# Linear attention and a squared-ReLU feed-forward layer: fourteen entries that copy weights to DRAM taken out, four moved, and the written order of all engines from step 17 on replaced

## Chip, cores, metric

The kernel runs on one NeuronCore of a Trainium2 chip. The metric is the device time of one execution in microseconds (us). Before the change three executions took 855.23, 855.45 and 857.17 us, so the median is 855.45 us.

## What is computed

```python
q_s = softmax of q over the head dimension          # q, k, v: 8 batches x 8 heads x 576 rows x 64
k_s = softmax of k over the sequence
kv  = einsum('bhsd,bhse->bhde', k_s, v)
x   = einsum('bhsd,bhde->bhse', q_s, kv)            # becomes 4608 tokens x 512
h   = x @ w_in                                      # w_in: 512 x 2048
out = (maximum(h, 0) ** 2) @ w_out                  # w_out: 2048 x 512
```

## The kernel before

**Blocks and steps.** Each batch is a block of 512 tokens; the 64 left over of each batch make a ninth block. A block's hidden units are worked on in 16 steps of 128. Blocks 0 to 2 are done step by step (steps 0 to 47): `h{n}_{cc}` is a quarter of the first product of step n, `relu`, `rm`, `ghi`, `glo` square it and split it into a rounded part and a rest, `o.{n}.{t}` is a quarter of the second product. Each h and each o is three matmuls of 128x512, since a product of two split numbers takes three. Blocks 3 and 4, 5 and 6, 7 and 8 are then done two at a time, in passes `s0`, `s1`, `s2`. There seven products of sums and differences of quarter matrices (`A11`, `S4`, `S2`, `A12`, `S3`, `S1`, `A22`, six matmuls each, for each of eight pieces) take the place of eight.

**What pass s0 needs.** The weights that all passes use are written to DRAM tensors and read back into a ring of seven tiles (`refill`, entries `s0.R.n`). The first use of the tile comes 10 to 25 us of matmuls after its entry. `ko{fc}` in the first list and `keep.{fc}` in the second are one copy of 512 KB of w_out (line 970). `WA{j}` and `w{j}.WA` are three copies of 256 KB of w_in (line 1030). The two inputs of pass s0 come back from DRAM (`x0.LB11`, `LB12`, `LB21`, `LB22`), their differences are `x0.T1` to `x0.T4`, and VectorE, ScalarE and GpSimd split each (`l`, `h`, `p`).

**Attention by pairs of heads.** A block has four pairs, written b.p (`2.1` is pair 1 of block 2). For a pair, `Lq`, `Lk`, `Lv` load it (two, two and four DMAs), `qm` to `qy` make the softmax of q, `tb` turns 32x32 pieces, `Bw` writes the result to one of two DRAM buffers `bounce` and `B` brings it back transposed as `qT` in four DMAs. `qh0`, `qh1` round the two heads' `qT` on ScalarE, `ql0`, `ql1` make the rests on GpSimd. `km`, `k1`, `k2`, `ke`, `kx` make the exponentials of k, `kv`, `kr`, `kh`, `kl` the small matrix, and `P0` to `P3` are the matmuls whose sums (`c`, `d`) are x. `XL` and `XR` store parts of x. In the first list the same things are called `Bw20`, `B20`, `qh20`, `kh20`, `kl20` and so on. `S0` to `S3` there store block 0's output, and `Lq23` loads the q of pair 2.3.

**The order.** Nothing is scheduled by a program. `ORDER` (line 51) covers the start up to step 17, `LIST` (line 92) the rest. Each entry issues its instructions, and every engine and the DMA queue of SyncE (SP) takes its own in exactly this order, since each instruction is issued after the one before it on the same engine:

```python
class InOrder:
    ...
                if self.last is not None:
                    order.enter_context(self.tc.issue_after(self.last.ins))
                ins = f(*args, **kwargs)
...
    def keep_out(fc):
        e.sp.dma_start(w_outs[fc], wo[fc].bitcast(F32))
...
    for token in LIST:
        run(token)
```

In the lists of before, `ORDER` copies w_out's chunks 0, 1, 2, 3, 4, 6, 7, 8 and w_in's groups 0 to 5, and `LIST` copies all thirteen and all eight.

Of the kernel before, what the change touches and what calls it, by code (L numbers as in the profile page):

```python
# [103 lines left out]
w0.h34 o.21.3 d0/2.2 B/2.3 h24_0 ghi23 P1/2.2 glo23 h24_1 c1/2.2 h24_2 w0.h12 d1/2.2 w4.WA w0.l34 xh0/2.2 P2/2.2
h24_3 c2/2.2 xl0/2.2 o.22.0 d2/2.2 relu24 tb/3.0 w0.l12 P3/2.2 w0.W34 o.22.1 rm24 k1/3.0 o.22.2 c3/2.2 qd/3.1
qh0/2.3 o.22.3 d3/2.2 w0.W12 h25_0 ghi24 ql0/2.3 kv/2.3 xh1/2.2 glo24 qh1/2.3 h25_1 kr/2.3 Bw/3.0 qx/3.1 xl1/2.2
h25_2 Lq/3.3 kh/2.3 ql1/2.3 qs/3.1 h25_3 o.23.0 Lv/3.1 relu25 o.23.1 kl/2.3 rm25 qy/3.1 k2/3.0 P0/2.3 o.23.2 c0/2.3
o.23.3 w1.a2 d0/2.3 h26_0 ghi25 tb/3.1 B/3.0 P1/2.3 h26_1 w1.s1 glo25 c1/2.3 h26_2 d1/2.3 kp/2.3 kz/3.0 ke/3.0
xh0/2.3 h26_3 Lk/3.1 P2/2.3 qm/3.2 xl0/2.3 o.24.0 relu26 Bw/3.1 o.24.1 w1.a1 rm26 XL/2.2 o.24.2 c2/2.3 qd/3.2 XL/2.3
kx/3.0 d2/2.3 o.24.3 qm/3.3 w3.WA P3/2.3 w1.s2 h27_0 ghi26 c3/2.3 glo26 h27_1 w1.s3 qh0/3.0 d3/2.3 h27_2 Lq/4.0  # L110
km/3.1 ql0/3.0 xh1/2.3 kv/3.0 qx/3.2 h27_3 Lv/3.2 kr/3.0 xl1/2.3 o.25.0 qs/3.2 relu27 w1.s4 o.25.1 rm27 o.25.2
k1/3.1 w1.h34 qy/3.2 o.25.3 w1.h12 B/3.1 h28_0 w1.l34 kp/3.0 ghi27 kz/3.1 h28_1 kh/3.0 glo27 w1.l12 h28_2 qm/4.0
w1.W34 h28_3 kl/3.0 o.26.0 w2.a1 relu28 P0/3.0 Lk/3.2 k2/3.1 rm28 o.26.1 c0/3.0 o.26.2 w1.W12 tb/3.2 P1/3.0 o.26.3
qh0/3.1 ke/3.1 h29_0 ghi28 w2.a2 Bw/3.2 h29_1 c1/3.0 glo28 XL/3.0 kx/3.1 h29_2 km/3.2 XR/3.0 ql0/3.1 h29_3 kv/3.1
relu29 k1/3.2 w1.WA w2.s1 o.27.0 rm29 o.27.1 w2.s2 kr/3.1 o.27.2 Lv/3.3 w2.s3 k2/3.2 kh/3.1 o.27.3 w2.s4 h30_0 ghi29
kl/3.1 h30_1 w2.h34 qd/3.3 glo29 P0/3.1 w2.h12 B/3.2 h30_2 w2.l34 kp/3.1 c0/3.1 h30_3 qx/3.3 w3.a1 P1/3.1 relu30
qs/3.3 w2.l12 o.28.0 Lq/4.1 rm30 o.28.1 c1/3.1 ke/3.2 o.28.2 w2.W34 o.28.3 qh0/3.2 qy/3.3 h31_0 ghi30 w2.W12 h31_1
ql0/3.2 kx/3.2 glo30 h31_2 qm/4.1 kv/3.2 tb/3.3 Lk/3.3 h31_3 kr/3.2 qd/4.0 o.29.0 relu31 XR/3.1 o.29.1 rm31 Bw/3.3
w3.a2 o.29.2 qx/4.0 Lq/4.2 o.29.3 kh/3.2 qs/4.0 w3.s1 h32_0 ghi31 Lv/4.0 h32_1 glo31 qy/4.0 h32_2 km/3.3 h32_3 w3.s2
o.30.0 tb/4.0 w3.s3 relu32 B/3.3 o.30.1 rm32 qm/4.2 qd/4.1 o.30.2 k1/3.3 o.30.3 w3.s4 Bw/4.0 h33_0 ghi32 Lq/4.3  # L120
kp/3.2 h33_1 qx/4.1 glo32 h33_2 w3.h34 qs/4.1 Lk/4.0 h33_3 w3.h12 o.31.0 k2/3.3 qy/4.1 XL/3.1 relu33 o.31.1 ev.1.0.a
x0.LB11 o.31.2 w3.l12 rm33 st.1.0 ev.1.1.d o.31.3 tb/4.1 h34_0 ghi33 w3.W12 ev.1.3.d qd/4.2 h34_1 glo33 h34_2 w3.l34
qx/4.2 h34_3 Bw/4.1 kl/3.2 o.32.0 w3.W34 relu34 ke/3.3 P0/3.2 o.32.1 ev.1.2.a qs/4.2 rm34 o.32.2 Lq/5.0 kx/3.3
km/4.0 qy/4.2 o.32.3 h35_0 st.1.1 ghi34 h35_1 c0/3.2 glo34 w4.a2 h35_2 XL/3.2 qm/4.3 st.1.2 P1/3.2 h35_3 w4.a1
qh0/3.3 o.33.0 k1/4.0 st.1.3 relu35 ql0/3.3 o.33.1 rm35 o.33.2 tb/4.2 c1/3.2 w6.WA w4.s1 kv/3.3 k2/4.0 w4.s2 o.33.3
XR/3.2 h36_0 w4.s3 kr/3.3 ghi35 Lv/4.1 h36_1 kp/3.3 kh/3.3 glo35 qd/4.3 h36_2 qm/5.0 h36_3 w4.s4 qx/4.3 o.34.0
kl/3.3 relu36 Lk/4.1 o.34.1 ke/4.0 rm36 P0/3.3 w4.h34 qs/4.3 o.34.2 Lq/5.1 c0/3.3 o.34.3 w4.h12 w4.l34 P1/3.3 XL/3.3
ghi36 h37_0 w4.l12 w4.W34 kx/4.0 glo36 h37_1 c1/3.3 km/4.1 h37_2 qy/4.3 kv/4.0 w4.W12 tb/4.3 h37_3 kp/4.0 o.35.0
kr/4.0 qd/5.0 relu37 o.35.1 XR/3.3 k1/4.1 rm37 Lk/4.2 o.35.2 w5.a2 kh/4.0 qx/5.0 o.35.3 k2/4.1 Lv/4.2 h38_0 ghi37
w5.s1 h38_1 glo37 h38_2 w5.a1 h38_3 kl/4.0 o.36.0 ke/4.1 B/4.0 relu38 o.36.1 km/4.2 w5.s2 rm38 o.36.2 kx/4.1 w5.s3  # L130
o.36.3 Lq/5.2 k1/4.2 w5.s4 h39_0 ghi38 h39_1 w5.h34 glo38 x0.LB21 h39_2 w5.l34 qh0/4.0 Bw/4.2 h39_3 k2/4.2 w5.h12
w5.W34 ql0/4.0 o.37.0 relu39 o.37.1 rm39 ke/4.2 o.37.2 B/4.1 P0/4.0 w6.a1 o.37.3 qm/5.2 w5.l12 h40_0 ghi39 h40_1
kx/4.2 glo39 w7.WA w6.a2 h40_2 c0/4.0 qs/5.0 h40_3 P1/4.0 qm/5.1 w5.W12 o.38.0 qy/5.0 qh0/4.1 o.38.1 relu40 o.38.2
ql0/4.1 tb/5.0 rm40 Bw/4.3 o.38.3 c1/4.0 XL/4.0 kv/4.1 ghi40 XR/4.0 B/4.2 h41_0 glo40 kp/4.1 w6.s1 h41_1 kr/4.1
h41_2 kh/4.1 w6.s2 Lk/4.3 h41_3 kl/4.1 w6.s3 o.39.0 Lv/4.3 P0/4.1 w6.s4 o.39.1 c0/4.1 w7.a1 o.39.2 relu41 P1/4.1
o.39.3 c1/4.1 w2.WA qh0/4.2 km/4.3 h42_0 kv/4.2 rm41 ql0/4.2 k1/4.3 ghi41 h42_1 XR/4.1 w6.h34 h42_2 Lv/5.0 w6.h12
glo41 h42_3 w6.l12 kr/4.2 o.40.0 relu42 k2/4.3 o.40.1 rm42 qd/5.1 o.40.2 B/4.3 kh/4.2 x0.hB110 o.40.3 kl/4.2 kp/4.2
h43_0 ghi42 ke/4.3 P0/4.2 w6.W12 glo42 kx/4.3 h43_1 w6.l34 h43_2 c0/4.2 h43_3 w6.W34 P1/4.2 relu43 o.41.0 kz/5.0
qh0/4.3 o.41.1 c1/4.2 Lk/5.0 ql0/4.3 o.41.2 rm43 kv/4.3 x0.hB111 XR/4.2 o.41.3 x0.hB210 kp/4.3 kr/4.3 Bw/5.0 h44_0
w7.a2 ghi43 Lk/5.1 h44_1 kh/4.3 glo43 h44_2 kl/4.3 s0.R.0 w7.s1 h44_3 km/5.0 Lv/5.1 P0/4.3 w7.s2 o.42.0 k1/5.0  # L140
c0/4.3 w7.s3 o.42.1 w7.s4 P1/4.3 k2/5.0 o.42.2 kz/5.1 c1/4.3 x0.LB12 relu44 o.42.3 XR/4.3 w7.h12 ke/5.0 h45_0 Lq/5.3
rm44 h45_1 km/5.1 w7.l12 w7.h34 h45_2 XL/4.3 ghi44 XL/4.1 h45_3 w7.l34 x0.hB211 w7.W12 o.43.0 glo44 relu45 o.43.1
# [1163 lines left out]
```

## Time and profile before

| | |
|---|---|
| median of three executions | 855.45 us |
| the profiled execution | 856.13 us |
| its span from first to last instruction | 854.3 us |
| time around the span | 1.83 us |
| mean granted TensorE clock | 0.997 |
| TensorE busy / VectorE / ScalarE / GpSimd | 837.1 / 548.8 / 494.0 / 287.0 us |
| bytes moved by all DMAs | 188.58 MB |
| written to HBM | 54.00 MB |

The span is what the engines took; the 1.83 us lie around it. TensorE (PE) has 4286 matmuls. Waits in which it sat idle can be found stretch by stretch.

### The profile page before, as it was taken

What the parts mean: (1) busy time and instruction counts of PE and PEld (TensorE: products, weight loads), DVE (VectorE), ACT (ScalarE), POOL (GpSimd) and SP (SyncE); (2) the same over time, 40 slices, a digit from 0 to 9 for tenths busy, and PEclk for the clock granted to TensorE, in tenths of its full rate; (3) what the DMA queues carried; (4) which work ended last, traced back from release to release, by engine and by line L of the source; (5) the groups of instructions that cost most, each with busy time, mean ns of one, the idle gap of its engine ahead of it and who ended that gap; (6) DMA issues with size and microseconds to landing.
All of it is one profiled execution on the core that took longest, in us unless ns stands there. A gap on an engine that the chain in (4) does not pass through costs nothing.

```text
span 854.3 us, 13089 instructions
## 1 busy us (share of the span) xinstructions
PE 837.1 (98%) x4286; PEld 679.1 (79%) x4286; DVE 548.8 (64%) x1153; ACT 494.0 (58%) x934; POOL 287.0 (34%) x275
## 2 busy tenths in 40 slices
...
GB/s 228 284 185 307 273 259 269 357 282 216 237 229 218 257 245 270 296 265 246 254 242 253 264 203 210 251 203 176 173 222 197 117 209 146 167 168 155 181 66 49
DMA packets 162643, 188.58 MB, mean 221 GB/s; under 512 B 52112, under 2 KB 125328, under 8 KB 162576
## 3 DMA queue, kind: packets, MB, share of 16 engines
...
q10 hardware_dynamic: 752, 0.95, 0.4%
...
HBM read 133.69 MB, written 54.00 MB: 220 GB/s over the span
## 4 chain that ended last, share of the span: by engine, by line
PE 84%; DVE 5%; DMA 4%; ACT 2%; issue 2%; SPq 2%; POOL 1%; DVEq 0%; ACTq 0%; POOLq 0%
PE bank L295 84%; DMA qt<-in_q_dram 2%; SPq L295 2%; DMA kt<-in_k_dram 1%; DVE m L295 1%; DMA xl_B<-x_raw 1%; DMA qT<-bounce 1%; DVE T L295 1%; DVE w L295 1%; DVE bank L295 1%; ACT bank L295 1%; DVE g_lo L295 0%; POOL qn L295 0%; ACT g_hi L295 0%; ACT qs L295 0%
## 5 line engine op out<-in xcount | busy, mean ns | idle before, releaser
L295 PE MATMUL bank<-wp,g 128*128 128x512 f32 x648 | 160.7, 390 | 0.0
L295 PEld LDWEIGHTS bank<-wp,g 128*128 128x128 f32 x648 | 120.8, 188 | 25.4
L295 PE MATMUL bank<-xh_T,wp 128*128 128x512 f32 x384 | 132.2, 393 | 1.1 <-ACT bank L295 1.1
L295 PE MATMUL bank<-x_hi,wi 128*128 128x512 f32 x384 | 132.5, 398 | 0.0
L295 PE MATMUL bank<-wo,g_hi 128*128 128x512 f32 x384 | 121.9, 399 | 0.0
L295 POOL TENSOR_TENSOR qs<-qT,qs 64x640 fp32r<-64x640 f32 (+1 forms) x40 | 62.7, 1568 | 105.9 <-ACT qs L295 88.5
L295 PE MATMUL bank<-xh_B,wp 128*128 128x512 f32 x288 | 98.0, 391 | 0.0
L295 DVE TENSOR_TENSOR c<-c,bank 128x512 f32<-128x512 f32 x48 | 33.0, 687 | 83.5 <-ACT c L295 83.3
L295 PEld LDWEIGHTS bank<-xh_T,wp 128*128 128x128 f32 x384 | 72.1, 188 | 17.5 <-ACT bank L295 1.9
L295 PEld LDWEIGHTS bank<-x_hi,wi 128*128 128x128 f32 x384 | 72.3, 188 | 16.4 <-DVE x_lo L295 0.4
L295 ACT ACTIVATE far<-far 128x512 f32<-128x512 f32 x96 | 60.7, 633 | 40.3 <-DVE far L295 38.8
L295 PEld LDWEIGHTS bank<-wo,g_hi 128*128 128x128 f32 x384 | 70.9, 190 | 14.9 <-ACT g_hi L295 0.4
L295 PE MATMUL bank<-wo,g_lo 128*128 128x512 f32 x192 | 75.8, 395 | 0.0
L295 PE MATMUL bank<-x_lo,wi 128*128 128x512 f32 x192 | 75.0, 391 | 0.0
L295 PE MATMUL bank<-xl_T,wp 128*128 128x512 f32 x192 | 74.8, 390 | 0.0
L295 PE MATMUL bank<-wo_back,g 128*128 128x512 f32 x288 | 72.0, 390 | 0.0
L295 DVE TENSOR_TENSOR far<-far,bank 128x512 f32<-128x512 f32 x48 | 32.9, 685 | 54.5 <-PE bank L295 54.4
L295 PEld LDWEIGHTS bank<-xh_B,wp 128*128 128x128 f32 x288 | 54.1, 188 | 11.6
L295 PEld LDWEIGHTS bank<-wo_back,g 128*128 128x128 f32 x288 | 53.7, 188 | 11.3
L295 DVE TENSOR_TENSOR g<-far,g 128x512 fp32r<-128x512 f32 x48 | 34.0, 747 | 38.7 <-ACT g L295 38.5
L295 ACT CAST g<-far 128x512 fp32r<-128x512 f32 x48 | 27.7, 620 | 51.5 <-PE bank L295 51.2
L295 PE MATMUL bank<-xl_B,wp 128*128 128x512 f32 x144 | 56.3, 391 | 0.0
(135 smaller groups left out, 1529.8 us busy)
## 6 DMA issues: line engine op xcount, KB each, us to landing
wp<-w_outs SPq DMA_DIRECT2D x54, 512.0 KB, 4.3
wp<-w_sums SPq DMA_DIRECT2D x96, 256.0 KB, 3.6
wp<-w_own SPq DMA_DIRECT2D x72, 256.0 KB, 3.5
w_own<-wi SPq DMA_DIRECT2D x42, 256.0 KB, 3.0
w_outs<-wo SPq DMA_DIRECT2D x21, 512.0 KB, 4.6
...
raw_i<-in_moe_w_in_dram SPq DMA_DIRECT2D x16, 512.0 KB, 7.1
raw_o<-in_moe_w_out_dram SPq DMA_DIRECT2D x16, 512.0 KB, 7.2
```

The lines of the kernel that those rows point to most:

```text
L295: ins = f(*args, **kwargs)
```

## The change

Only the two lists change. `ORDER` loses `ko7`, `ko8` and `WA5`, `ko0`, `ko1` and `ko3` stand earlier and `ko6` later. `LIST` loses `keep.0`, `.1`, `.2`, `.3`, `.4`, `.6` and `w0.WA` to `w4.WA`. Each weight is then copied once: chunks 0, 1, 2, 3, 4, 6 and groups 0 to 4 in `ORDER`, the others in `LIST`. In `LIST` the same 2686 other entries stand in a new order; its last 429 entries are the same. `w5.WA`, `w6.WA`, `w7.WA` now stand between steps 21 and 22; before, w6 and w7 stood near steps 35 and 40.

```diff
 s2o10 hii12 loi12 relu11 Lo12 Lv20 lowi13 qs13 qadd13 ti13 kexp20 lowi14 Lo15 Lq21 o8_0 o9_0 s1i13 hio10 loo10 rs13
-rr13 kvn13 s2i13 rm11 lowo14 Lv21 WA0 WA1 to11 o8_2 o9_2 ghi10 ghi11 h12_0:0 h12_1 h12_2 h12_3 rc13 qmul13 s1o11
...
-h15_0:3 h15_1 h15_2 h15_3 Lv22 WA2 WA3 ko0 ko1 ko2 ghi13 relu14 to14 s1o14 s2o14 to15 glo13 o13_3 o13_1 o13_2 hio14
-loo14 o13_0 s1o15 s2o15 hio15 rm14 ghi14 glo14 h16_0:1 relu15 rm15 ghi15 glo15 Bw20 Lk23 WA4 ko3 ko4 ko6 ko7 o14_3
-qsub21 at13:3 loo15 o15_3 xhi13 xlo13 o14_0 o15_0 B20 rs20 h16_1 rr20 qexp21 ev3 S3 qn21 ev0 S0 WA5 ko8 Bw21 h16_2
-o14_1 o15_1 ev1 qh20 ql20 kf20 h16_3 relu16 rm16 ghi16 S1 B21 glo16 o14_2 o15_2 ev2 S2 kh20 kl20 Lq23 h17_0:3 h17_1
...
+rr13 kvn13 s2i13 rm11 lowo14 Lv21 WA0 WA1 ko0 ko1 to11 o8_2 o9_2 ghi10 ghi11 h12_0:0 h12_1 h12_2 h12_3 rc13 qmul13
...
+h15_0:3 h15_1 h15_2 h15_3 Lv22 WA2 WA3 ko2 ko3 ghi13 relu14 to14 s1o14 s2o14 to15 glo13 o13_3 o13_1 o13_2 hio14
+loo14 o13_0 s1o15 s2o15 hio15 rm14 ghi14 glo14 h16_0:1 relu15 rm15 ghi15 glo15 Bw20 Lk23 WA4 ko4 o14_3 qsub21 at13:3
+loo15 o15_3 xhi13 xlo13 o14_0 o15_0 B20 rs20 h16_1 rr20 qexp21 ev3 S3 qn21 ev0 S0 ko6 Bw21 h16_2 o14_1 o15_1 ev1
...
 LIST = """
-w0.a2 w0.s1 qm/2.2 P0/2.0 h18_0 relu17 km/2.2 qd/2.2 h18_1 rm17 h18_2 ghi17 c0/2.0 h18_3 glo17 qx/2.2 o.16.0 d0/2.0
-relu18 qs/2.2 P1/2.0 o.16.1 rm18 o.16.2 c1/2.0 qy/2.2 Lq/3.0 d1/2.0 o.16.3 k1/2.2 P2/2.0 h19_0 ghi18 keep.9 c2/2.0
-h19_1 glo18 xh0/2.0 keep.11 h19_2 xl0/2.0 d2/2.0 keep.0 tb/2.2 h19_3 keep.12 P3/2.0 keep.1 o.17.0 qm/2.3 relu19
-Bw/2.2 o.17.1 rm19 k2/2.2 qd/2.3 keep.13 o.17.2 c3/2.0 keep.15 o.17.3 d3/2.0 qx/2.3 Lq/3.1 ke/2.2 h20_0 ghi19 kv/2.1
-kx/2.2 glo19 keep.2 h20_1 keep.3 xh1/2.0 qs/2.3 qh0/2.1 xl1/2.0 Lv/2.3 h20_2 qh1/2.1 h20_3 kr/2.1 qy/2.3 o.18.0
-km/2.3 relu20 o.18.1 ql0/2.1 rm20 tb/2.3 o.18.2 keep.4 kh/2.1 keep.6 o.18.3 kp/2.1 Bw/2.3 kl/2.1 h21_0 ghi20 ql1/2.1
-keep.7 P0/2.1 glo20 h21_1 keep.8 c0/2.1 h21_2 XL/2.0 d0/2.1 k1/2.3 P1/2.1 h21_3 c1/2.1 o.19.0 d1/2.1 relu21 o.19.1
-k2/2.3 XL/2.1 rm21 P2/2.1 o.19.2 c2/2.1 xh0/2.1 o.19.3 d2/2.1 B/2.2 xl0/2.1 qm/3.0 P3/2.1 h22_0 ghi21 qd/3.0 c3/2.1
-glo21 h22_1 d3/2.1 h22_2 w0.WA ke/2.3 xh1/2.1 kv/2.2 xl1/2.1 kx/2.3 h22_3 kr/2.2 Lq/3.2 kp/2.2 o.20.0 w0.a1 relu22
-o.20.1 rm22 qm/3.1 w0.s2 Lk/3.0 o.20.2 qh0/2.2 w0.s3 o.20.3 kh/2.2 ql0/2.2 Lv/3.0 h23_0 ghi22 h23_1 qh1/2.2 glo22
...
-k2/5.1 kh/5.0 Lk/5.2 h46_3 o.44.0 kl/5.0 relu46 s0.R.2 x0.T10 o.44.1 rm46 Lv/5.2 x0.lB110 o.44.2 x0.hT10 o.44.3
...
-x0.hT11 x0.T31 o.46.2 o.46.3 x0.lT11 x0.hT31 s0.0.A11 x0.hB221 x0.pT40 glo47 back.0 o.47.0 x0.T21 x0.pB210 x0.hT21
-s0.0.c1 back.1 ev.2.0.a x0.lT21 st.2.0 x0.T41 s0.0.S2 kx/5.1 x0.lT31 x0.hT41 km/5.2 x0.pB211 s0.R.7 s0.0.u2 x0.pT41
...
+w0.a2 w0.s1 h18_0 relu17 qm/2.2 P0/2.0 h18_1 rm17 km/2.2 qd/2.2 h18_2 ghi17 h18_3 c0/2.0 glo17 o.16.0 relu18 d0/2.0
+o.16.1 km/2.3 rm18 P1/2.0 o.16.2 c1/2.0 o.16.3 qx/2.2 d1/2.0 Lq/3.0 P2/2.0 qs/2.2 ghi18 h19_0 c2/2.0 h19_1 keep.9
+xh0/2.0 glo18 keep.11 qy/2.2 h19_2 keep.12 d2/2.0 h19_3 keep.13 xl0/2.0 tb/2.2 P3/2.0 o.17.0 relu19 keep.15 k1/2.2
+o.17.1 Bw/2.2 rm19 keep.7 o.17.2 c3/2.0 qh0/2.1 keep.8 d3/2.0 o.17.3 qm/2.3 XL/2.0 ql0/2.1 kv/2.1 ghi19 xh1/2.0
+h20_0 glo19 Lv/2.3 qh1/2.1 qd/2.3 h20_1 k2/2.2 h20_2 xl1/2.0 qx/2.3 h20_3 k1/2.3 ql1/2.1 o.18.0 Lq/3.1 relu20 o.18.1
+kr/2.1 rm20 o.18.2 ke/2.2 kp/2.1 kh/2.1 B/2.2 o.18.3 k2/2.3 h21_0 ghi20 h21_1 kx/2.2 glo20 h21_2 w5.WA qs/2.3 h21_3
+o.19.0 relu21 kl/2.1 o.19.1 ke/2.3 rm21 P0/2.1 w6.WA o.19.2 qm/3.0 qy/2.3 c0/2.1 o.19.3 kx/2.3 d0/2.1 h22_0 tb/2.3
...
+glo44 h45_3 ke/5.1 o.43.0 x0.LB22 relu45 tb/5.1 o.43.1 rm45 x0.T10 Bw/5.1 o.43.2 kx/5.1 o.43.3 x0.lB110 x0.hT10
+h46_0 s0.R.1 ghi45 x0.lT10 h46_1 glo45 qd/5.2 h46_2 km/5.2 x0.hB220 h46_3 back.1 Lq/6.0 o.44.0 x0.T30 relu46 o.44.1
...
+x0.hT31 x0.lT11 B/5.0 o.46.0 ghi47 x0.lT31 o.46.1 glo47 x0.pT40 o.46.2 s0.R.5 o.46.3 x0.T21 s0.0.A11 x0.T41 x0.hT21
+x0.lT21 back.2 o.47.0 s0.0.c1 qs/5.2 x0.pB211 ev.2.0.a s0.0.S2 x0.hT41 st.2.0 k1/5.2 x0.pT41 s0.0.A12 s0.0.u2 s0.R.7
...
```

Some distances in the two lists, in the matmul time that stands between two entries (each matmul at the rate that the profile shows, three to an h or o, six to a product):

| from, to | before, us | after, us |
|---|---|---|
| B/2.2 to qh0/2.2 | 5.6 | 13.5 |
| start of LIST to qh0/2.2 | 29.1 | 30.5 |
| x0.LB22 to x0.T30 | 6.1 | 5.5 |
| start of LIST to x0.T30 | 177.7 | 173.7 |
| start of LIST to s0.0.S2 | 185.9 | 185.9 |
| Lk/6.1 to km/6.1 | 5.8 | 5.8 |
| Lk/5.0 to km/5.0 | 4.8 | 4.5 |
| Lk/5.1 to km/5.1 | 6.9 | 5.6 |
| Lk/7.1 to km/7.1 | 5.7 | 4.9 |
| Lq/6.3 to qm/6.3 | 15.5 | 4.3 |
| B/5.1 to Bw/5.3 | 7.5 | 3.4 |

In blocks 5 to 7, eight loads of k or q stand 7.0 us or less ahead of their first user before, and eleven after.

## Rows read from the trace of the kernel before

**Rows 1.** The page's first part: busy time of each engine.
```profile
PE 837.1 (98%) x4286; PEld 679.1 (79%) x4286; DVE 548.8 (64%) x1153; ACT 494.0 (58%) x934; POOL 287.0 (34%) x275
```

**Rows 2.** Busy time by stretch; after the engines: granted clock, DMA share, GB/s.
```profile
135.00:142.00 7.00, 5.60 (x26) 4.37 (x25) 4.14 (x8) 6.22 (x13) 5.24 (x5) 1.00 0.95 296
157.00:162.00 5.00, 3.53 (x16) 2.49 (x14) 4.80 (x11) 3.51 (x9) 4.51 (x5) 1.00 1.02 384
162.00:174.00 12.00, 12.00 (x71) 9.73 (x71) 7.65 (x22) 5.63 (x11) 4.53 (x6) 1.00 0.97 344
174.00:181.00 7.00, 3.18 (x13) 2.37 (x12) 2.45 (x3) 4.51 (x10) 3.62 (x3) 0.93 0.84 248
181.00:184.00 3.00, 3.00 (x9) 2.33 (x9) 2.90 (x6) 1.39 (x4) 1.43 (x2) 0.59 0.68 178
334.00:342.00 8.00, 6.83 (x29) 5.02 (x28) 7.17 (x15) 4.95 (x9) 2.99 (x4) 1.00 0.81 244
418.00:424.00 6.00, 4.91 (x23) 3.81 (x22) 4.47 (x15) 3.07 (x6) 0.00 (x0) 1.00 1.05 316
600.00:700.00 100.00, 100.00 (x443) 82.52 (x442) 43.69 (x62) 44.01 (x77) 9.15 (x6) 1.00 0.57 180
```

**Rows 3.** What PE waited for: us in total, times, longest.
```profile
PE bank L295 <- DVE kvs L295: 3.8, 1, 3.8
PE bank L295 <- POOL kt L295: 1.5, 1, 1.5
...
PE bank L295 <- DVE xr L295: 1.1, 1, 1.1
```

**Rows 4.** The chain that ended last: start, us, what.
```profile
148.50 3.06 DMA qt<-in_q_dram
...
174.68 2.10 DMA qT<-bounce
...
321.40 5.92 DMA xl_B<-x_raw
...
337.55 0.59 ACT bank L295
...
414.37 4.78 DMA kt<-in_k_dram
```

**Rows 5.** SP's queue in order of time: start, us of issuing, DMAs.
```profile
101.47 3.85 SPq L295 DMA_DIRECT2D w_own<-wi  x6
107.44 1.27 SPq L295 DMA_DIRECT2D qt<-in_q_dram  x2
...
126.76 4.00 SPq L295 DMA_DIRECT2D w_outs<-wo  x4
130.87 3.42 SPq L295 DMA_DIRECT2D qT<-bounce  x4
...
136.91 1.67 SPq L295 DMA_DIRECT2D w_own<-wi  x3
...
147.79 2.73 SPq L295 DMA_DIRECT2D qt<-in_q_dram  x4
150.57 4.41 SPq L295 DMA_DIRECT2D w_outs<-wo  x5
155.08 1.16 SPq L295 DMA_DIRECT2D bounce<-tb  x1
...
173.27 1.84 SPq L295 DMA_DIRECT2D qT<-bounce  x4
```

**Rows 6.** The page's DMA issues: KB each, us to landing.
```profile
w_own<-wi SPq DMA_DIRECT2D x42, 256.0 KB, 3.0
w_outs<-wo SPq DMA_DIRECT2D x21, 512.0 KB, 4.6
```

**Rows 7.** VectorE's groups by form: busy us, mean ns, idle before.
```profile
L295 DVE TENSOR_TENSOR T<-xl_B,T 128x512 f32<-128x512 f32 x12 | 8.2, 685 | 0.1
...
L295 DVE TENSOR_TENSOR T<-xl_T,xl_B 128x512 f32<-128x512 f32 x6 | 6.3, 1046 | 0.0
```

More of the change, by code (lines that the diff above doesn't have):

```diff
@@ L89 @@
+h15_0:3 h15_1 h15_2 h15_3 Lv22 WA2 WA3 ko2 ko3 ghi13 relu14 to14 s1o14 s2o14 to15 glo13 o13_3 o13_1 o13_2 hio14
+loo14 o13_0 s1o15 s2o15 hio15 rm14 ghi14 glo14 h16_0:1 relu15 rm15 ghi15 glo15 Bw20 Lk23 WA4 ko4 o14_3 qsub21 at13:3
+loo15 o15_3 xhi13 xlo13 o14_0 o15_0 B20 rs20 h16_1 rr20 qexp21 ev3 S3 qn21 ev0 S0 ko6 Bw21 h16_2 o14_1 o15_1 ev1
+qh20 ql20 kf20 h16_3 relu16 rm16 ghi16 S1 B21 glo16 o14_2 o15_2 ev2 S2 kh20 kl20 Lq23 h17_0:3 h17_1 h17_2 h17_3
 """.split()
 LIST = """
-w0.a2 w0.s1 qm/2.2 P0/2.0 h18_0 relu17 km/2.2 qd/2.2 h18_1 rm17 h18_2 ghi17 c0/2.0 h18_3 glo17 qx/2.2 o.16.0 d0/2.0
@@ L104 @@
[L104 to L142, printed above, removed]
-k1/5.1 rm45 o.43.2 kx/5.0 w7.W34 o.43.3 kv/5.0 ghi45 h46_0 glo45 qx/5.1 kp/5.0 s0.R.1 h46_1 kr/5.0 x0.LB22 h46_2
```

316 lines of the change are left out of this document (178 added, 138 removed).

## Prediction

> **What bounds the kernel now.** Read the busy times first [rows 1]: PE is busy 837.1 of 854.3 us, so all its idle time is 17.2 us, and some of that lies at the start and at the end. No other engine is near the span. So the question is only in which stretches PE stands still, and whether the new lists end those waits. Next read the stretches [rows 2]. From 600 to 700 us PE runs without a gap, 443 matmuls in 100 us, 0.226 us each; that is the pace when nothing is late. Five stretches have a gap: 135 to 142 (7.00 - 5.60 = 1.40 us), 157 to 162 (1.47), 174 to 181 (3.82), 334 to 342 (1.17) and 418 to 424 (1.09). After the third gap in which PE stood still for 3.82 us, the granted clock falls from 2.4 GHz to its lower level of 1.2 GHz for a while: 0.93 and 0.59 of full on average in two stretches, that is, 0.07 x 7 + 0.41 x 3 = 1.72 us at which PE does no work although it counts as busy. The first three gaps with this loss are 8.41 us; all together are 10.67 us.
>
> Then ask what came last at each gap. The waits [rows 3] name small things: VectorE's `kvs` (3.8), GpSimd's `kt` (1.5), VectorE's `xr` (1.1). The chain [rows 4] shows what made these late: behind the third gap the return of the bounced q for pair 2.2 (`qT<-bounce`), behind the second the load of q for pair 2.3, which VectorE waited for at the head of its order, so that everything after it was late. Both are DMAs of SP's queue. Now read that queue [rows 5]: from 126 to 175 us it issues almost without a pause. `Bw/2.2` went out at 155.08, but its partner `B/2.2` only at 173.27, behind weight copies. The DMAs moved 344 and 384 GB/s at shares of 0.97 and 1.02 [rows 2], so the queue is full because the DMAs are.
>
> **The change, part by part.**
>
> *Copies removed.* Counts must fall from 42 to 24 for w_in and from 21 to 13 for w_out [rows 6]: 18 x 256 KB + 8 x 512 KB = 8.9 MB less. No reader waits for a second copy, so nothing else goes.
>
> *First gap, -1.40.* P0/2.0 waits for kh20, which stands behind qh20, which waits for `B20`. Before, four w_out copies (4.00 us of issuing) stand right ahead of `B20` at 130.87 [rows 5]; one is left, so B20 goes out some 3.0 us earlier. That is 1.6 us more than needed. What would be late next is kh20 behind step 16's relu16, rm16 and ghi16 on ScalarE, which wait for PE itself. The two copies moved to the place behind WA1 go into a pause: WA0 and WA1 are issued at 105.3 (101.47 + 3.85), the next load at 107.44 [rows 5], and two copies take 2.0.
>
> *Second gap, -1.47.* Ahead of `Lq23`, which goes out at 147.79, ko7, ko8 and WA5 are gone: about 1.00 (a quarter of 4.00), the same at most, and 1.67 us [rows 5], 3 us in all. Besides, in the new list `ql0/2.1`, which P0/2.1 needs, stands ahead of pair 2.3's work on GpSimd, no longer behind it. What would be late next is kl/2.1, and P0/2.1 stands 3.4 us of matmuls later than before.
>
> *Third gap, -3.82, and the clock, -1.72.* Between the start of LIST and `B/2.2` thirteen w_out copies were queued, now seven. Six of 0.524 MB are 3.1 MB, at the 344 GB/s of the stretch 9.1 us; the 1.8 MB gone ahead of LIST are 5.3 us more. `B/2.2` must come 3.82 us earlier relative to qh0/2.2, and in the list itself it now stands 13.5 us of matmuls ahead of it, where it stood 5.6. The loss of clock came only after this longest gap; the gaps of 1.40 and 1.47 left it at 1.00 [rows 2]. So it goes with the gap. Bounds: all 5.54 us, or, if half the lateness stays, 1.91 us and no loss of clock after it, 3.63 us; I take all of it.
>
> *w5, w6, w7 moved forward.* Nine copies of 0.262 MB, 2.4 MB, 6.9 us at 344 GB/s. They stand behind `B/2.2`; next behind them are Bw/2.3 and Lq/3.2, whose users are 13 and 6 us of matmuls away. I cost them at nothing; if that cover is gone, one load waits as in the last gap, 1.1 us.
>
> *Start of pass s0.* The gap at 334 ends with ScalarE's copy at 337.55 [rows 4], behind a chain of differences on VectorE from x0.T30 on. T30 needs the load x0.LB22, which took 5.92 us. T30 moves 4.0 us forward in the list and S2 stays, but LB22 moves only 3.4, and two more VectorE instructions stand in between (2 x 0.69). Gain at most 3.4 - 1.4 = 2.0, more than the gap; at least nothing, if LB22 lands 5.92 us after its place, since T30 stands 5.5 behind it. Half of the gap: -0.6.
>
> *The gap at 418.* VectorE waits for `Lk/6.1` (414.37, 4.78 us [rows 4]) and then PE for xr [rows 3]. The distance to its user is 5.8 us in both lists, with the same loads just ahead. I leave it: 0.
>
> *The rest of the new order.* It removes and adds no instruction besides the copies, but changes what stands ahead of what. Nearest row for a load placed too close: 1.09 us. Four stand at under 5.7 us and closer than before (Lk/5.0, Lk/5.1, Lk/7.1, Lq/6.3), so between 0 and 4.4 us. Before, Lk/5.0 stood at 4.8 and PE had no gap there, so the low end is nearer; I take one, +1.1. New too: `bounce` has two buffers, and Bw/5.3 now stands 3.4 us behind B/5.1, whose reads must be done. SP waits there, and behind it stand refills with some 19 us to spare, so 0.
>
> *GpSimd beside VectorE.* One difference of two SBUF tiles takes 685 ns on average, the same shape elsewhere 1046 [rows 7], a loss of 0.36 us on average that depends on what GpSimd does then. The new order shifts every such meeting; I cost the change in them at nothing on balance. The Trainium skill (SBUF — State Buffer, "SBUF: two separate sides") says that VectorE with two SBUF inputs and GpSimd take turns on one port pair, and the loser "fully blocks". The trace agrees as far as these two rows go.
>
> **Sum.** -1.40 - 1.47 - 3.82 - 1.72 - 0.6 + 1.1 = -7.9 us. The profiled execution took 856.13 us (its span of 854.3 and 1.83 around it), so 848.2. The median of the three runs lies 0.68 below that execution, so 847.5 us.
>
> **Rivals.**
>
> *All gaps go.* 10.67 us off the median: 844.8. For it: in both later gaps something moved forward or is less loaded. Against it: Lk/6.1's distance is the same.
>
> *Loads too close.* All four cost 1.09: 847.5 + 3.3 = 850.8. For it: the gap at 418 is just such a load. Against it: 4.8 us sufficed before.
>
> *GpSimd and VectorE meet in bad places.* If nine more instructions on the path lose the 0.36 us: 847.5 + 3.2 = 850.7. For it: the two rows of one shape. Against it: the new lists may as well part instructions that met. By the Trainium skill (SBUF — State Buffer, "SBUF: two separate sides") it would happen wherever a GpSimd instruction and a VectorE one with two SBUF inputs now stand side by side.
>
> *The change does not thin the queue where it matters.* Up to Bw/2.3 there were 13 w_out copies, and now there are seven and six w_in copies ahead of it, three more just behind. If half of the third gap and all of the second stay: 847.5 + 1.91 + 1.47 = 850.9; if the third stays whole with its clock, 847.5 + 5.54 + 1.47 = 854.5, no measurable change. Against it: `B/2.2` stands ahead of those six.
>
> *Slower.* Loads of k and q late throughout blocks 5 to 7: eleven stand at 7.0 us or less from their users. One is in the gap at 418 already and one in the sum, so nine are left. At 1.09 us each they end at 857.3, within 0.3%; it is slower from 1.17 each on (858.0), and if each cost the 1.6 us by which a landing of 5.92 exceeds the shortest distance of 4.3, 861.9. For it: a DMA share of 1.05 at 418 [rows 2]. Against it: of the eight such loads before, one shows a gap.
>
> **How the numbers follow.** Forecast (845.3 to 849.7, a load's wait of 1.09 more or less twice) 0.51; all gaps go 0.13; close loads 0.13, of it 0.04 with more such that end within 0.3% of before; GpSimd and VectorE 0.08; queue not thinned 0.09, of it 0.04 within 0.3%; slower 0.06. 0.3% of 855.45 is 2.6 us, about what a measurement of this kernel can tell from no change, so faster means under 852.9. Faster: 0.51 + 0.13 + 0.09 + 0.08 + 0.05 = 0.86; same 0.08; slower 0.06. The range runs from all gaps gone with some smaller lateness besides (10.67 and 1.3: 843.5) to 853.0, which holds the rivals that end near 851; it leaves out the slower case and those within 0.3%, 0.14.
>
> **What would show it.** PE without gaps from 135 to 184 us and a granted clock of 1.00 there; `B20` near 128 and `B/2.2` near 160 us; w_own x24 and w_outs x13, 179.7 MB moved. A gap of about 1 us where Lk/6.1 lands, and at most half of one at the start of pass s0. The forecast is wrong if a gap of over 2 us stands anywhere between 190 and 600 us, above all in blocks 5 to 7 with a k or q load at its head, or if SP still issues without a pause up to 175.

## The result and the profile after

The kernel after takes 845.05 us (median of four runs, 844.96 to 845.31), beside 855.34 us for the kernel before on the same chip: a ratio of 0.9878, 95% interval [0.9861, 0.9895]. That is faster, by 10.3 us. It lies inside the predicted range, 2.5 us below the predicted time. It is 0.25 us under the forecast's own band (845.3 to 849.7, held at 0.51) and almost at the 844.8 us of the rival "all gaps go" (held at 0.13). Run again beside the last experiments it took 845.18 us (ratio 0.9883 [0.9858, 0.9908]). One of the four executions of the experiment e8_567_late, the profiled one, took 1389.76 us at a granted clock of 0.557 and is left out of every number below.

The profiled execution has a span of 843.2 us. First its busy times, the row that answers to [rows 1]:

```profile
PE 835.2 (99%) x4286; PEld 678.8 (80%) x4286; DVE 551.5 (65%) x1153; ACT 494.6 (59%) x934; POOL 288.0 (34%) x275
```

The span is 11.1 us shorter. PE's idle time fell from 17.2 to 8.0 us, which is 9.2, and its busy time by 1.9 us with the same 4286 matmuls: most of that is the time at the lower clock, which I had put at 1.72. Of the 9.2 us the five gaps make 8.95; before 135 us PE was idle 0.50 us less as well (132.01 us busy, 131.51 before), and one new wait of 0.22 us stands between 424 and 500 us. The stretches that had a gap in [rows 2], now (the work in them is shifted by some 10 us in the later ones):

```profile
135.00:142.00 7.00, 7.00 (x32) 5.78 (x31) 6.92 (x11) 5.39 (x13) 4.70 (x4) 1.00 0.80 238
157.00:162.00 5.00, 5.00 (x23) 4.11 (x23) 4.86 (x10) 2.97 (x5) 1.27 (x1) 1.00 0.65 160
174.00:181.00 7.00, 7.00 (x33) 5.79 (x32) 4.89 (x11) 5.77 (x13) 3.95 (x3) 1.00 0.74 216
181.00:184.00 3.00, 3.00 (x15) 2.46 (x15) 2.80 (x9) 1.56 (x5) 2.64 (x3) 1.00 0.82 235
...
322.00:330.00 8.00, 8.00 (x36) 6.32 (x35) 7.59 (x22) 4.12 (x8) 2.59 (x2) 1.00 0.91 266
402.00:408.00 6.00, 6.00 (x28) 4.91 (x28) 4.79 (x10) 3.42 (x7) 2.52 (x2) 1.00 0.97 262
```

322 to 330 holds the start of pass s0 and 402 to 408 the landing of `Lk/6.1`. PE is busy all the time in each, and the granted clock is 1.00 (2.4 GHz). DMA still has shares of 0.65 to 0.97, but the stretch 157 to 162 fell from 1.02 and 384 GB/s to 0.65 and 160. The chain of work that ended last has one piece of PE alone from 128 to 180 us, where [rows 4] had two DMAs (start, us, what), and PE's waits have lost `kvs`, `kt` and the 1.1 us of `xr` of [rows 3]:

```profile
127.77 52.39 PE bank L293 x261
```

```profile
PE bank L293 <- POOL x_hi L293: 1.3, 1, 1.3
PE bank L293 <- DVE qs L293: 0.6, 1, 0.6
PE bank L293 <- ACT ke L293: 0.5, 1, 0.5
PE bank L293 <- POOL qn L293: 0.2, 1, 0.2
PE bank L293 <- DVE xr L293: 0.2, 1, 0.2
```

SP's queue, beside [rows 5], and the DMA issues, beside [rows 6]:

```profile
126.63 1.01 SPq L293 DMA_DIRECT2D w_outs<-wo  x1
128.97 1.81 SPq L293 DMA_DIRECT2D qT<-bounce  x4
...
141.90 3.55 SPq L293 DMA_DIRECT2D qt<-in_q_dram  x4
145.50 4.43 SPq L293 DMA_DIRECT2D w_outs<-wo  x5
150.35 0.83 SPq L293 DMA_DIRECT2D bounce<-tb  x1
...
159.49 1.96 SPq L293 DMA_DIRECT2D qT<-bounce  x4
161.50 3.82 SPq L293 DMA_DIRECT2D w_own<-wi  x6
```

```profile
w_outs<-wo SPq DMA_DIRECT2D x13, 512.0 KB, 4.3
w_own<-wi SPq DMA_DIRECT2D x24, 256.0 KB, 3.2
```

One copy stands ahead of `B20`. SP reached it at 127.75 us, waited there 1.2 us, and issued it at 128.97 (130.87 before); its last part landed at 132.46 (136.19 before). The other two: `Lq23` went out at 141.90 (147.79), `B/2.2` at 159.49 (173.27), 9.1 us behind `Bw/2.2` and no longer 18.2.

### The profile page after: what moved, and what is told of

The parts are those of the page before. It is cut to its first block, busy times and chain, and to the rows that moved or that the text cites. A ratio compares the mean times of both kernels' runs of the same rounds, so it can differ in the third digit from the quotient of the medians.

```text
span 843.2 us, 13068 instructions
## 1 busy us (share of the span) xinstructions
PE 835.2 (99%) x4286; PEld 678.8 (80%) x4286; DVE 551.5 (65%) x1153; ACT 494.6 (59%) x934; POOL 288.0 (34%) x275
## 2 busy tenths in 40 slices
DMA packets 156595, 179.66 MB, mean 213 GB/s; under 512 B 51696, under 2 KB 120304, under 8 KB 156528
## 4 chain that ended last, share of the span: by engine, by line
PE 93%; DMA 3%; DVE 2%; POOL 0%; ACT 0%; issue 0%; SPq 0%; DVEq 0%; POOLq 0%
PE bank L293 93%; DMA kt<-in_k_dram 1%; DMA vt<-in_v_dram 1%; DVE m L293 1%; DMA qt<-in_q_dram 1%; SPq L293 0%; POOL wi L293 0%; DVE r L293 0%; DVE w L293 0%; ACT qn L293 0%; DVE bank L293 0%; POOL qn L293 0%; DVE qs L293 0%; DVE ke L293 0%; DVE o L293 0%
## 5 line engine op out<-in xcount | busy, mean ns | idle before, releaser
L293 POOL TENSOR_TENSOR qs<-qT,qs 64x640 fp32r<-64x640 f32 (+1 forms) x40 | 64.5, 1613 | 102.0 <-ACT qs L293 92.7
L293 PEld LDWEIGHTS bank<-xh_B,wp 128*128 128x128 f32 x288 | 54.1, 188 | 11.7
L293 DVE TENSOR_TENSOR g<-far,g 128x512 fp32r<-128x512 f32 x48 | 31.9, 702 | 41.7 <-ACT g L293 41.7
L293 POOL TENSOR_TENSOR qn<-qt,qm 128x640 f32<-128x640 f32 x30 | 40.3, 1345 | 53.9 <-DVE tb L293 31.8
```

## The experiments

The theory to test was the prediction's: the three early gaps and the lower clock came from second copies in SP's queue. Its rival: they came from the order, above all from the place of `B/2.2`. For the two later gaps the prediction had no firm reason, so those were open. The kernels ran in three groups of four (e1 to e4, e5 to e8, e9 to e12), each on one chip, where the kernel before took 856.8, 855.66 and 855.59 us. Unless said otherwise, an experiment only moves or leaves out tokens of the two lists. Gaps are read from one profiled execution of each. Apart from e3_late_old the experiments without any second copy end at ratios of 0.9885 to 0.9899, with intervals that overlap those of the kernel after: the gaps in the traces tell them apart, and the times do not.

**e1_copies_only**: before, less the second copies.

```diff
 ORDER  -ko7 -ko8 -WA5
 LIST   -keep.0 -keep.1 -keep.2 -keep.3 -keep.4 -keep.6 -w0.WA -w1.WA -w2.WA -w3.WA -w4.WA
```

> The old order of ORDER and LIST, with only the fourteen second copies left out and nothing moved. Theory (the copies made SP's queue late): the three gaps up to 181 us and the loss of clock are gone, 8.41 us, and the gaps at the start of pass s0 and at Lk/6.1 (1.17 + 1.09) stay: 855.3 - 8.4 = 846.9. Rival (B/2.2 stands too close to its user, copies or not): the third gap of 3.82 us with its 1.72 us of clock stays, the two smaller ones go: 855.3 - 2.9 = 852.4.

Measured: 848.51 us, ratio 0.9899 [0.9882, 0.9917], 8.3 us faster with nothing moved. Stretches of its trace (columns as in [rows 2]):

```profile
136.00:142.00 6.00, 4.97 (x23) 3.83 (x22) 4.50 (x5) 4.81 (x12) 4.76 (x5) 1.00 0.75 207
154.00:162.00 8.00, 8.00 (x37) 6.61 (x36) 6.42 (x19) 4.97 (x12) 4.55 (x4) 1.00 0.64 218
162.00:184.00 22.00, 22.00 (x132) 17.79 (x131) 17.03 (x37) 16.50 (x35) 15.25 (x15) 1.00 0.62 182
327.00:335.00 8.00, 6.83 (x29) 5.01 (x28) 7.08 (x18) 5.10 (x9) 3.87 (x3) 1.00 0.86 265
411.00:417.00 6.00, 4.90 (x22) 3.77 (x21) 4.91 (x16) 3.14 (x6) 0.00 (x0) 1.00 0.90 274
```

Second and third gap and the loss of clock are gone without any new order. 1.03 us of the first gap stay (three copies are still ahead of `B20`; e11_order_copies and e4_early_old, with the same three, keep 0.39 and 0.53), and both late gaps stay whole, 1.17 and 1.10. That speaks for the theory and against the rival: `B/2.2` stands no further ahead of its user than before.

**e2_order_only**: the other half, after with the second copies put back.

```diff
 ORDER  S0 ko6 +WA5 +ko7 +ko8
 LIST   keep.11 +keep.0   keep.12 +keep.1   +keep.2 +keep.3 Lv/2.3   +keep.4 kh/2.1 +keep.6
        c3/2.1 +w0.WA   d1/2.2 +w4.WA   qm/3.3 +w3.WA   k1/3.2 +w1.WA   k2/4.1 +w2.WA
```

> The new order, with the fourteen second copies put back beside the neighbours that they had (keep.4 and keep.6 ahead of B/2.2, as before; ko7, ko8 and WA5 behind B20). Theory (copies): the first gap stays away, since only one copy stands ahead of B20, but the second (1.47 us) comes back, and the third with its clock in part or whole: 845.05 + 1.47 + 1.91 to 5.54 = 848.4 to 852.1. Rival (order): 845.1, since B/2.2 stands 13.5 us of matmuls ahead of its user.

Measured: 862.68 us, ratio 1.0067 [1.0047, 1.0086]: slower than before, which neither theory expected. Two stretches and VectorE's timeline (start, us, instruction, idle before):

```profile
180.00:190.00 10.00, 1.17 (x6) 0.74 (x5) 3.30 (x9) 2.89 (x8) 2.11 (x3) 0.79 0.95 295
190.00:194.00 4.00, 4.00 (x14) 3.22 (x14) 2.13 (x4) 2.53 (x6) 1.50 (x1) 0.67 0.81 224
```

```profile
185.60 0.82 DVE L289 TENSOR_REDUCE qm<-qt 128x10 f32<-128x640 f32 x1 [8.22 <-DMA qt<-in_q_dram]
```

PE is idle for 8.83 of 10 us, and VectorE waited 8.22 us for `Lq/3.2`, issued at 181.53 behind w5.WA, w6.WA and w7.WA. The first gap stayed away, as expected, since only one copy stands ahead of `B20`; in place of the two others stand one of 2.54 us at 171 and this one. So the new order alone does not make the gain: with the second copies in these places it costs 6 us.

**e7_dup_567_late**: e2_order_only with those three copies back at their old places.

```diff
 LIST   -w5.WA -w6.WA -w7.WA (behind B/2.2)   o.21.0 +w5.WA   c1/3.2 +w6.WA   glo39 +w7.WA
```

> As e2_order_only (new order, second copies put back), but with w5.WA, w6.WA and w7.WA at their old places. Theory (in e2_order_only their nine transfers, 6.8 us of issuing, stood ahead of Lq/3.2, for which VectorE and then PE waited 9.0 us): most of that gap goes, 862.7 - 6.8 = 855.9, less some 1.4 us of clock. Rival (the fourteen second copies alone make it): 862.7.

Measured: 861.93 us, ratio 1.0076 [1.0055, 1.0097]. `Lq/3.2` landed 6.1 us earlier (179.38 and 185.51) as expected, but the sum failed: in its place stand gaps of 2.84 us in two pieces between 180 and 192, 1.74 between 196 and 202 and 2.98 at 273 (row below), with the clock at 0.54 behind the last. The last stands behind a second copy too: SP issued `w2.WA` (three transfers) at 266.59 and a load of v behind it, through which the chain that ended last runs there. With the second copies in, taking one load out of the jam left others in it.

```profile
271.00:277.00 6.00, 3.02 (x13) 2.36 (x12) 2.00 (x3) 3.16 (x7) 1.02 (x1) 0.87 0.86 253
277.00:279.00 2.00, 2.00 (x7) 1.57 (x6) 1.96 (x3) 1.64 (x5) 0.00 (x0) 0.54 0.75 230
```

**e8_567_late**: the same move, but in the kernel after, without second copies.

> The kernel after, with w5.WA, w6.WA and w7.WA at their old places. Theory (their nine transfers are hidden early as they were late): 845.1. Rival (early they cost something near Lq/3.2 that is now saved): 844 or less. Second rival (late they collide with the refills): one or two loads' waits of 1.1 us more, 846 to 847.

Measured: 845.64 us (median of three), ratio 0.9885 [0.9868, 0.9903], beside 0.9878 and 0.9883 for after: no difference that can be told. With the second copies gone, no price shows for where these nine transfers stand, as far as an interval 3 us wide can tell.

**e11_order_copies**: how much of the removal is needed. Before without ko7, ko8 and WA5; LIST's second copies stay.

> The kernel before with only ko7, ko8 and WA5 left out (five transfers, 1.8 MB), the eleven second copies of LIST still there. Theory (every byte ahead of B/2.2 counts alike, 1.8 MB are 5.3 us, more than the gap of 3.82): second and third gap and the loss of clock go, as in e1_copies_only, 848.5. Rival (the copies between Bw/2.2 and B/2.2 are needed for it): the third gap stays with its clock, 854.0, or half of it without, 850.4.

Measured: 849.39 us, ratio 0.9928 [0.9901, 0.9954]. That lies between theory and rival. Three tokens of ORDER give 6.2 of the 10 us:

```profile
136.00:142.00 6.00, 5.61 (x26) 4.38 (x25) 4.46 (x6) 4.95 (x13) 5.43 (x5) 1.00 0.73 208
154.00:162.00 8.00, 8.00 (x37) 6.61 (x36) 6.77 (x20) 5.19 (x13) 4.00 (x4) 1.00 0.99 332
162.00:184.00 22.00, 21.28 (x127) 16.82 (x126) 16.00 (x34) 15.45 (x32) 13.98 (x14) 1.00 0.86 274
```

The third gap shrank to 0.72 us and the clock stayed. `B/2.2` landed at 170.91 us (176.78 before), 5.9 us earlier for 1.8 MB, where the prediction had 5.3. In e1_copies_only, with another 3.1 MB gone from LIST, it landed at 165.29, 5.6 us earlier again, where the prediction had 9.1: the DMA share of 154 to 162 us was 0.99 before that second step and 0.64 after it. SP's queue in e1_copies_only shows what held `B/2.2` there: the two stores of x just ahead of it take 3.91 us, since the second waits until 161.28 for the part that VectorE makes, and `B/2.2` follows at 161.76. SP waited for an engine, so fewer bytes ahead of `B/2.2` could no longer bring it forward.

```profile
157.76 3.91 SPq L288 DMA_DIRECT2D x_left<-xf  x2
161.76 1.83 SPq L288 DMA_DIRECT2D qT<-bounce  x4
```

**e3_late_old** and **e4_early_old**: new order up to step 24 of the main loop and old behind it, and the reverse; no second copies in either.

> The new order up to step 24 of the main loop, from there on the old one; no second copy. Theory (the gaps at the start of pass s0 and at Lk/6.1 end by the new order of the late part): both come back, 845.05 + 2.26 = 847.3. Rival (they went because the early part runs without gaps and meets other DMA traffic): 845.1.

> The old order up to step 24, without the second copies, from there on the new one. Theory (the copies alone made the early gaps): 845.1, as the kernel after. Rival (B/2.2's place is needed): the third gap stays whole with its clock, 845.05 + 5.54 = 850.6, or half of it, 847.0.

e4_early_old took 846.98 us (0.9886 [0.9871, 0.9900]): no gap in 154 to 184 with the old early order, none at the start of pass s0, 0.15 at `Lk/6.1`, 0.53 of the first gap, and a new one of 1.17 us at 441, behind `Lk/6.3`, which landed 5.8 us after its issue (5.2 in the kernel after).

```profile
154.00:184.00 30.00, 30.00 (x152) 24.59 (x151) 24.41 (x51) 19.43 (x41) 17.27 (x17) 1.00 0.78 245
325.00:333.00 8.00, 8.00 (x35) 6.31 (x34) 6.42 (x21) 4.84 (x8) 4.91 (x4) 1.00 0.66 191
```

e3_late_old took 852.13 us (0.9942 [0.9924, 0.9960]), 4.8 more than expected, and its ten runs spread from 848.5 to 855.1. The two late gaps came back, 1.14 us (330 to 336) and 2.28 (414 to 420), the last with a clock of 0.51 behind it. The rest is the seam: at the cut `km/3.0` came to stand ahead of `d0/2.2` on VectorE, waited for its load, and PE stood still for 2.05 us at 176 with 0.50 of the clock behind that.

```profile
176.00:181.00 5.00, 2.95 (x13) 1.97 (x12) 4.01 (x8) 2.81 (x7) 0.00 (x0) 0.96 0.64 179
181.00:184.00 3.00, 3.00 (x9) 2.42 (x8) 2.24 (x9) 2.56 (x6) 2.25 (x3) 0.50 0.47 175
...
330.00:336.00 6.00, 4.86 (x21) 3.36 (x19) 5.32 (x8) 4.49 (x8) 1.68 (x2) 1.00 0.76 250
414.00:420.00 6.00, 3.72 (x16) 2.79 (x15) 3.99 (x14) 2.33 (x6) 0.00 (x0) 0.96 0.97 286
420.00:423.00 3.00, 3.00 (x8) 2.30 (x7) 2.66 (x6) 1.19 (x2) 0.00 (x0) 0.51 0.81 232
```

The two together show that the late gaps belong to the late part of the order.

**e5_two_forward**: which edits of that order end them? Old LIST without second copies, new ORDER, two loads moved.

```diff
 LIST   o.43.1 +x0.LB22 ... h46_1 kr/5.0 -x0.LB22
        s0.o.6.3 +B/5.3 ... k2/6.0 -B/5.3
```

> The old order of LIST without second copies, with the new ORDER (one copy ahead of B20 where e1_copies_only has three) and two loads moved forward: x0.LB22 by some 3.5 us of matmuls, B/5.3 from just ahead of Lk/6.1's neighbours to step 6 of pass s0. Theory (each of the three gaps that e1_copies_only kept has this one cause): 848.5 - 1.2 - 1.3 - 1.3 = 844.7, as the kernel after, with almost all of its new order left out. Rival (the late gaps need the rest of the new order): 847.3.

Measured: 846.34 us, ratio 0.9897 [0.9876, 0.9919], between theory and rival, and the stretches say why:

```profile
136.00:142.00 6.00, 6.00 (x29) 4.97 (x28) 5.94 (x10) 5.03 (x12) 3.42 (x4) 1.00 0.76 236
326.00:332.00 6.00, 4.83 (x21) 3.34 (x20) 5.25 (x9) 4.31 (x8) 2.36 (x2) 1.00 0.70 232
404.00:412.00 8.00, 8.00 (x38) 6.47 (x37) 6.14 (x14) 4.85 (x9) 2.09 (x2) 1.00 0.93 286
```

The first gap went with ORDER's moved copies (two fewer ahead of `B20`), and the one at `Lk/6.1` with `B/5.3`, the only edit near it. The one at pass s0 stayed, 1.17 us, although `x0.LB22` now landed at 315.03, 3.5 us before T30 began. So the load was not its cause here. VectorE's timeline, with GpSimd's below it, shows another: VectorE works without a pause from T30 to T21, and T11 and lB111 (the rows at 321.70 and 323.51) take 1.78 and 1.67 us where their like take 0.69, while GpSimd runs pT40 and pB210.

```profile
318.57 0.68 DVE L288 TENSOR_TENSOR T<-xl_B,xl_T 128x512 f32<-128x512 f32 x1
...
321.70 1.78 DVE L288 TENSOR_TENSOR T<-xl_T,xl_B 128x512 f32<-128x512 f32 x1
323.51 1.67 DVE L288 TENSOR_TENSOR xl_B<-xl_B,xh_B 128x512 fp32r<-128x512 f32 x1
```

```profile
321.37 1.56 POOL L288 TENSOR_TENSOR xl_T<-T,xh_T 128x512 fp32r<-128x512 f32 x1 [9.29 <-ACT xh_T L288]
322.89 1.74 POOL L288 TENSOR_TENSOR xl_B<-xl_B,xh_B 128x512 fp32r<-128x512 f32 x1
```

**e9_pool_apart**: so part them. Its result is not the program's: it makes the first half of T4 from the low part of B21 in place of B21, since the split now comes first. Its instructions are the same.

```diff
 LIST   x0.hB211 +x0.pB210 ...  -x0.pT40 ... -x0.pB210 ... x0.lT21 +x0.pT40
```

> As e5_two_forward, with GpSimd's x0.pB210 moved 14 us earlier and x0.pT40 some 6 us later, so that neither runs beside VectorE's T11 and lB111 (1.78 and 1.67 us there, 0.69 for their like elsewhere). Theory (these two, and not the load LB22, keep the gap of 1.30 us at the start of pass s0): both take 0.69, the chain ends 2.1 us earlier, the gap goes: 846.3 - 1.3 = 845.0. Rival (T30's place behind ke/5.1 and g_lo of step 46 sets it): no change, 846.3.

Only half of the edit took hold: GpSimd has nothing else to do there, so pT40 began as soon as its input was there, at 322.94, and again met T11. pB210 ran at 308.59.

```profile
323.26 1.78 DVE L288 TENSOR_TENSOR T<-xl_T,xl_B 128x512 f32<-128x512 f32 x1
325.08 0.69 DVE L288 TENSOR_TENSOR xl_B<-xl_B,xh_B 128x512 fp32r<-128x512 f32 x1
```

```profile
327.00:333.00 6.00, 5.75 (x25) 4.09 (x23) 5.19 (x10) 4.18 (x9) 2.76 (x2) 1.00 0.85 278
```

lB111 fell by 0.98 us and the gap by 0.92, from 1.17 to 0.25, so for that half the cause is shown; T11, the other half, kept its 1.78 us and is not tested. The time, 846.55 us (ratio 0.9896 [0.9866, 0.9926]), does not show the 0.9 us: its interval is 5 us wide, and in the profiled execution PE stood still for 1.70 us at 17 us, for a load of v that the edit does not touch.

**e6_two_back**: the reverse of e5_two_forward, in the kernel after.

```diff
 LIST   o.43.0 -x0.LB22 ... h46_0 +x0.LB22     -B/5.3 s0.o.6.3 ... k2/6.0 +B/5.3
        qh0/5.3 ql0/5.3 qh1/5.3 ql1/5.3 behind it, at their old places
```

> The kernel after, with x0.LB22 moved 2.7 us of matmuls later, and B/5.3 with the splits that read it put back to their old places. Theory: the gaps at the start of pass s0 and at Lk/6.1 come back, about 1.2 and 1.1 us: 847.3. Rival (LB22 has 1.5 us of slack and B/5.3 is not what made Lk/6.1 late): 845.1 to 846.2.

Measured: 846.49 us, ratio 0.9895 [0.9879, 0.9911]. No gap at pass s0: LB22 went out only 1.3 us later, and T30 began at 315.85, 11.7 us ahead of the copy c1 of S2's bank (9.6 before, 12.2 after). Nor was `Lk/6.1` late. PE did lose 1.11 us between 400 and 408, for another reason: ql0/5.3 and ql1/5.3 now ran on GpSimd beside VectorE's kl/5.3, whose two small differences took 3.22 us there, and 0.46 in the kernel after. VectorE's row, and GpSimd's:

```profile
400.64 3.22 DVE L289 TENSOR_TENSOR kvs<-kf,kvs 64x64 fp32r<-64x64 f32 x2
```

```profile
400.38 3.39 POOL L289 TENSOR_TENSOR qs<-qT,qs 64x640 fp32r<-64x640 f32 x2 [2.29 <-ACT qs L289]
```

So in the old order `B/5.3` ahead of it made `Lk/6.1` late; in the new one it does not, although much the same transfers stand between the two. What else in the new order brings `Lk/6.1` forward is not shown.

**e10_loads_late** and **e12_after_again**: the price of a load that stands too close.

> The kernel after with Lk/5.0, Lk/5.1, Lk/7.1 and Lq/6.3 each moved 2.0 to 2.4 us of matmuls later. Theory (the new order holds them just far enough): Lk/5.1 and Lk/7.1 landed 1.8 and 1.7 us ahead of their users and cost little, Lk/5.0 and Lq/6.3 have nothing to spare at VectorE and cost 1 to 2.4 us each: 847 to 850. Rival (VectorE's wait is hidden from PE, so places this close cost nothing): 845.1.

> The kernel after as it is, once more, beside the other three: 845.1, without a gap of over 0.5 us behind 130 us.

Measured: 845.88 us for the four loads later (0.9895 [0.9865, 0.9925]) and 845.18 for after itself on that chip, 0.7 us and not 2 to 5: nearly the rival's answer. Two of the four hardly went out later: `Lk/5.0` was issued at 287.58 (287.16 in the first profile of after) and `Lk/5.1` at 295.88 (295.81), since in both kernels SP reaches them only behind a run of other issues. So only two places were tested. `Lk/7.1` went out 1.6 us later and `Lq/6.3` 3.1, and PE shows 0.13 us of idle time from 382 to 386. 0.41 us more stand between 408 and 412, where `Lk/6.1` landed later.

How late `Lk/6.1` is can be read over thirteen traces: its issue and its landing, both from the start of step 8 of pass s0 on PE, and by how much the matmul that needs it then came late (us, worked out from each trace from start to start, 0.16 more than the idle time above; "-" is under 0.15).

```
                  B/5.3 issued   Lk/6.1 issued   landed   PE late
e12_after_again      -15.3           -0.06         4.54      -
after                -15.2           -0.05         4.61      -
e6_two_back           -7.8           -0.23         4.94      -
e2_order_only        -15.4            0.24         5.05      -
e7_dup_567_late      -15.0            0.33         5.51      -
e5_two_forward       -14.3            0.47         5.58      -
e9_pool_apart        -13.1            0.47         5.59      -
e4_early_old         -15.0           -0.05         5.79     0.31
e10_loads_late       -14.8            0.19         6.06     0.57
e11_order_copies     -11.1            0.49         6.50     0.90
before               -10.9            1.42         6.85     1.25
e1_copies_only       -11.1            1.08         6.87     1.25
e3_late_old          -11.1            1.91         8.11     2.44
```

Where PE is late, it is late by the landing less 5.5 to 5.7 us. Two things add up in the landing: when SP issues (-0.23 to 1.91 us) and the 4.6 to 6.2 us from issue to landing. The place of `B/5.3` alone sets neither: e5_two_forward and e11_order_copies issue `Lk/6.1` at the same time, with `B/5.3` 3.2 us apart, and e6_two_back issues it first of all, with `B/5.3` last of all. What sets the time from issue to landing stays open.

## Why the prediction was right, and which of its terms were not

**Copies, and the three early gaps with the clock: right.** 24 and 13 issues, 179.66 MB moved, and all of 1.40 + 1.47 + 3.82 + 1.72 us gone. e1_copies_only gives most of it from the removal alone, and e2_order_only, with the order alone, ends only the first gap, where fewer copies stand ahead of `B20`. `B20` was to go out 3.0 us earlier; SP was there 3.1 us earlier, waited 1.2 and issued it 1.9 us earlier. It landed 3.7 us earlier, since its four issues took 1.81 us and no longer 3.42. That is more than the gap needed. Of the bytes, the first 1.8 MB were priced well (5.3, measured 5.9) and the next 3.1 MB too high (9.1, measured 5.6), because the price of a full queue was used up to a point where SP waited for VectorE instead. Together they were enough: needed were the 3.82 us and the 2.87 by which PE itself came earlier, 6.7, and 11.5 were there. In e11_order_copies, which kept 0.39 of the first gap, 6.3 were needed and 5.9 there, and 0.72 of the gap stayed.

**The rival "the change does not thin the queue where it matters" fell.** It counted the six copies behind `B/2.2`, and e8_567_late finds no price for them. (Its first count is off as well: eleven w_out copies stood ahead of `Bw/2.3` before, and thirteen ahead of `B/2.2`.) e2_order_only shows that the sentence "if that cover is gone, one load waits, 1.1 us" was too mild: with the queue full the wait was 8.22 us.

**The start of pass s0: half the mechanism, half the size.** The term was -0.6, its gap went whole, 1.17 us. The step that failed is "T30 needs the load x0.LB22", taken as the one thing that sets T30, with the gain bounded by how far that load moves and then halved. With the old late order VectorE's own order set T30: the load had landed 0.65 us ahead of it before and 3.5 us ahead in e5_two_forward, where moving the load alone gave nothing. In the kernel after, T30 does wait for the load, 0.23 us (row below), but both now stand early enough: T30 begins 12.2 us ahead of c1 and no longer 9.6. The lengthening of T11 and lB111 stood in [rows 7] as a mean of 1046 ns and was costed at nothing on balance; e9_pool_apart puts 0.92 us of this gap on one of the two. In the kernel after T11 and lB111 take 0.68 and 0.69 us, and GpSimd meets lT30 instead (1.76 us), which is hidden with T30 2.6 us further ahead. How much of the gap the earlier start ended, and how much the parted meetings, is not shown.

```profile
315.05 0.69 DVE L293 TENSOR_TENSOR T<-xl_B,xl_T 128x512 f32<-128x512 f32 x1 [0.23 <-DMA xl_B<-x_raw]
```

The Trainium skill (SBUF — State Buffer, "SBUF: two separate sides") calls the shared port pair an exclusive lock held for the whole instruction. e6_two_back agrees: two differences that take 0.23 us each alone took 1.58 and 1.61 beside two GpSimd instructions of 1.76 and 1.56, and each ended 0.08 to 0.09 us after the GpSimd instruction beside it.

**The gap at `Lk/6.1`: left at 0, measured -1.09.** The step that failed is "the distance to its user is 5.8 us in both lists, with the same loads just ahead". Distance in the list is not when SP issues: `Lk/6.1` went out 1.42 us after step 8 began, and 0.05 before it in the kernel after, and took 4.7 us to land and no longer 5.4, so that, counted from step 8, it landed 2.2 us earlier. The gap of about 1 us that I had named as a sign did not appear. `B/5.3` with its four transfers had moved away from just ahead, which I did not count; e5_two_forward shows that this is enough in the old order, e6_two_back that it is not needed in the new one.

**Close loads: +1.1, measured nothing.** In the kernel after PE has no idle time from 135 to 424 us and 0.22 us from there to 500. The step that failed is the price: it took one gap of before for what a place in the list costs. In e10_loads_late two such loads went out 1.6 and 3.1 us later still, and the medians differ by 0.7 us, less than the intervals can tell.

With these three terms as measured the sum is -1.40 - 1.47 - 3.82 - 1.72 - 1.17 - 1.09 = -10.67, the rival "all gaps go". I had held against it only that `Lk/6.1`'s distance was the same. All three errors point the same way, so the total owes nothing to errors that cancel; it lay in the range because the range held that rival.
